# Packed chunks of attention: where the parts of keys and queries and the memory product are made

## The chip, the cores and the metric

The kernel runs on one core of a Trainium2 chip. The time is device microseconds of that core. The engines are named PE (TensorE), DVE (VectorE), ACT (ScalarE), POOL (GpSimd) and SP (SyncE, which issues most DMAs). Each takes its own instructions in the order in which they were issued to it; semaphores order them across engines.

## The reference

Attention with a memory term, and a top-2 mixture of experts on its result. B = 4 batches, H = 8 heads, S = 576 rows, D = 64; 2304 tokens of 512 values; 8 experts with 512 x 1024 and 1024 x 512 weights.

```
scores = q @ k^T / 8, causal; a = softmax(scores); local = a @ v
q_p    = where(q > 0, q, exp(q) - 1) + 1
mem    = (q_p @ M_prev) / (q_p . z_prev + 1e-6)
x      = sigmoid(beta) * mem + (1 - sigmoid(beta)) * local
logits = x @ w_gate + log1p(exp(x @ w_noise)) * noise; the two largest, softmax over them
out    = sum over the two experts of weight * (relu(x @ w1[e]) @ w2[e])
```

All is float32.

## The kernel before

**Precision.** A product that must be near float32 is made of three products of split operands: a high part (a copy into fp32r) and a low part (the float32 value minus the high part): high x high, low x high, high x low. So each operand needs one cast and one subtraction before it can be used.

**Attention.** A batch has 576 rows: four chunks of 128 rows (i = 0 to 3) and one of 64 (i = 4). Chunks are numbered c = 0 to 19, so the last ones of the batches are c = 4, 9, 14 and 19. These are packed: the 64 rows of two heads share the 128 partitions (`q4` tiles with zeros off the diagonal, one pair for all packed chunks), and their scores are made at line 519, with 576 keys in two halves of 288. The first half needs keys of older chunks only; the second needs the chunk's own 64 keys. Other chunks make their scores at line 528.

A chunk is worked in units of heads, two heads each for i of 2 or more. A step of the main loop (line 738) handles unit u: the exponentials of unit u + 1 (`expo`, line 559), the products with the values of unit u - 2 (`av`, line 599), the score products of unit u + 2 (`score`: `products`, then `tops`, which adds the mask and takes each row's negated maximum at line 538), and the transposes of unit u (`trans`, lines 577 and 578). Between them go the steps that prepare later chunks, by due times (lines 706 to 715): `q_turn` and `q_split`, `k_turn` with `k_split`, `q_min`, `phi`, `mem`. `in_turn` (line 726) ties TensorE's instructions to each other in exactly the order in which the steps were issued. The other engines keep the order of issue by their queues.

**The steps that the change touches.** `k_turn` transposes the keys on PE (line 409), ACT scales them into `kf` (line 416), and `k_split` makes the high part (line 421) and the low part (line 422) in the tile `kT`. `q_turn` makes `qf` (line 441); `q_split(0)` makes the high part (line 452) and `q_split(1)` the low part (line 454), for a packed chunk in two pieces of 64 x 256. `mem` makes the memory product, twice in a chunk with four heads each: PE (line 466), a copy by ACT (line 469), the divisor by DVE (lines 473 and 475), and the product into `xm` (line 476), which `out_turn` adds at line 639. From chunk 2 on, lines 421, 422, 452, 454 and 476 all run on POOL.

**Routing.** A finished chunk is scaled on DVE (lines 637 and 639), transposed (line 149) and multiplied with the gate weights (lines 160, 161); when a batch is finished, `routing` counts places with small DVE steps (line 196 and others), and writes ten rows of a table to DRAM by indirect DMAs that POOL issues (`put`, line 282). The steps of batch b are worked while batch b + 1 is in attention, and its puts fall into that batch's later chunks. After the puts of batch 2, `early` (line 837) loads the first table rows (`tabE`, by SP) and POOL gathers rows of x by them (`xw`, line 809); the experts' part begins with these (`xprep`, line 855).

**Experts.** Nine passes over the weights; PE makes lines 919 and 932, DVE, ACT and POOL split weights (lines 880 to 883), POOL gathers and scatters rows.

Of the kernel before, what the change touches and what calls it, by code (L numbers as in the profile page):

```python
# [9 lines left out]
F32 = mybir.dt.float32  # L10
# [5 lines left out]
ALU = mybir.AluOpType  # L16
# [25 lines left out]
def rows_of(i):  # L42
    return P if i < 4 else 64
# [3 lines left out]
def tile_attention_moe(ctx: ExitStack, tc: tile.TileContext, q, k, v, M_prev, z_prev, beta,  # L47
                       w_gate, w_noise, noise, w1, w2, out):
    nc = tc.nc
# [269 lines left out]
    def attention():  # L319
        with ExitStack() as c2:  # L320
# [71 lines left out]
            def prep(c):  # L392

                b, i = chunks[c]
                n = rows_of(i)
                d = CH.setdefault(c, {"b": b, "i": i, "n": n})
                t0 = i * P

                def keys():

                    if i == 0:
                        KT[b] = (ap_ if b % 2 else kp).tile([P, 2, 4, S], F32R, tag="kT", name="kT", bufs=1)
                    return [KT[b][:, x_, :, t0:t0 + n] for x_ in range(2)]
# [9 lines left out]
                def k_turn():  # L413
                    v_ = turn("k")
                    d["kf"] = ap_.tile([P, 4, P], F32, tag="kf", name="kf", bufs=2)[:, :, 0:n]
                    nc.scalar.activation(d["kf"], v_, AF.Copy, scale=0.125)
                    k_split()

                def k_split():
                    hi, lo = keys()  # L420
                    (nc.gpsimd.tensor_copy if c > 1 else nc.scalar.copy)(hi, d["kf"])
                    nc.gpsimd.tensor_tensor(out=lo, in0=d["kf"], in1=hi.bitcast(F32), op=ALU.subtract)

                def turn_first(nm, g0):

# [21 lines left out]
                def q_split(part):  # L447
                    for j in ([0, 1] if i == 4 else [None]):
                        a = slice(0, P) if j is None else slice(j * 64, j * 64 + 64)
                        hi, lo = [d[nm][a, :, a] for nm in ("qh", "ql")]  # L450
                        if part == 0:
                            (nc.gpsimd.tensor_copy if c > 1 else nc.scalar.copy)(hi, d["qf"][a])
                        else:
                            nc.gpsimd.tensor_tensor(out=lo, in0=d["qf"][a], in1=hi.bitcast(F32), op=ALU.subtract)

                def q_min():
                    d["qpT"] = ap_.tile([P, 4, P], F32, tag="qpT", name="qpT", bufs=2)
# [2 lines left out]
                def mem(g0):  # L460
                    if g0 == 0:
                        d["xm"] = ap_.tile([P, H, D], F32, tag="xm", name="xm", bufs=4)
                    tp = ps_tp.tile([P, 512], F32, tag="tp", name="tpm")
                    v_ = tp[0:n, 0:4 * 65].rearrange("p (h e) -> p h e", e=65)
                    for g in range(2):
                        nc.tensor.matmul(tp[0:n, g * 130:(g + 1) * 130], d["qpT"][:, g0 + g, 0:n],
                                         mz[:, b, g0 + g].rearrange("p a e -> p (a e)"), start=True, stop=True)
                    m_ = ap_.tile([P, 4 * 65], F32, tag="mm", name="mm", bufs=3)
                    nc.scalar.copy(m_[0:n], tp[0:n, 0:4 * 65])
                    v_ = m_[0:n].rearrange("p (h e) -> p h e", e=65)  # L470
                    r = ap_.tile([P, 4, 1], F32, tag="mr", name="mr", bufs=4)
                    hs = slice(2 * g0, 2 * g0 + 4)
                    nc.vector.scalar_tensor_tensor(out=r[0:n], in0=v_[:, :, 64:65], scalar=1e-6, in1=ig[0:n, hs].unsqueeze(2),
                                                   op0=ALU.add, op1=ALU.mult)
                    nc.vector.reciprocal(r[0:n], r[0:n])
                    nc.gpsimd.tensor_tensor(out=d["xm"][0:n, hs, :], in0=v_[:, :, 0:64],
                                            in1=r[0:n].to_broadcast([n, 4, 64]), op=ALU.mult)

                mm = [lambda: mem(0), lambda: mem(2)]
                qk = [lambda: q_split(0), lambda: q_split(1)]  # L480
                if c == 0:
                    return ([lambda nm=nm, g0=g0: turn_first(nm, g0) for g0 in (0, 2) for nm in "kq"],
# [255 lines left out]
            for u in range(NU + 2):  # L738
# [14 lines left out]
                if u < NU:  # L753
                    c, hs = units[u]
# [39 lines left out]
            d = CH[len(chunks) - 1]  # L794
# [413 lines left out]
```

## Time and profile before

| | |
|---|---|
| median of 3 runs | 780.79 us (780.27 to 782.5) |
| the profiled execution | 776.3 us, of which the span from first to last instruction is 774.6 |
| PE busy | 708.3 us, 91% |
| DVE | 418.1 us, 54% |
| ACT | 370.9 us, 48% |
| POOL | 364.2 us, 47% |

The page shows the span in 40 slices of 19.4 us. A digit is the busy share in tenths; PEclk is the granted clock of TensorE in tenths of full speed.

```profile
PE   6999995999599949988999999999999999999994
...
POOL 5534436433655360646453472662752753723602
PEclk7899997999799979999999999999999999999998
```

Read it by columns: in the 7th, 11th and 15th slice PE is only half busy and its clock is lower. Attention fills the first 16 slices, the experts the others. A timeline shows start and length of each instruction, or of a few of one kind; what stands in brackets is the engine's idle time before it and what released it.

### The profile page before, as it was taken

The page shows a single profiled execution, that of the slowest core. Times are in us where ns is not written, and L with a number is a line of the kernel's source. Part 1 is how long each engine was busy: PE and PEld are TensorE (multiplying, and loading weights), DVE is VectorE, ACT ScalarE, POOL GpSimd, SP SyncE. Part 2 cuts the span into 40 slices and gives each one's busy share as a digit, 9 for nine tenths or more (in the row PEclk, how much of TensorE's full clock was granted, in tenths as well). Part 3 has the DMA queues.
Part 4 walks back from the last instruction along what each step waited for, and adds up shares of the span by engine and source line. Part 5 has one row for each costly group of instructions (what it writes and reads, how often), then busy time and mean ns, then how long its engine had stood idle before and what let it go on. Part 6 is the DMA issues. An engine that isn't in the chain of part 4 may idle for free. (4 is left out here: it accounts for less than half of the span.)

```text
span 774.6 us, 14494 instructions
## 1 busy us (share of the span) xinstructions
PE 708.3 (91%) x5166; PEld 610.2 (79%) x5166; DVE 418.1 (54%) x1053; ACT 370.9 (48%) x951; POOL 364.2 (47%) x400
## 2 busy tenths in 40 slices
PE   6999995999599949988999999999999999999994
PEld 4778774877477737777888899988899888898883
DVE  3766683578367825945546454464554555455212
ACT  4887873797368736315525225235144144153110
POOL 5534436433655360646453472662752753723602
PEclk7899997999799979999999999999999999999998
DMA  8663521241120012559658466575594693864301
GB/s 162 104 145 89 112 56 36 62 97 55 36 63 22 29 41 84 153 120 224 192 106 208 143 150 162 161 191 119 183 200 106 191 213 111 219 146 144 101 1 61
DMA packets 165919, 92.95 MB, mean 120 GB/s; under 512 B 110564, under 2 KB 145380, under 8 KB 165840
## 3 DMA queue, kind: packets, MB, share of 16 engines
q1 hardware_dynamic: 155760, 72.97, 38.5%
q0 software_dynamic: 10080, 18.98, 9.7%
q8 instruction: 43, 0.70, 0.4%
q14 instruction: 36, 0.29, 0.1%
HBM read 69.68 MB, written 22.54 MB: 119 GB/s over the span
## 5 line engine op out<-in xcount | busy, mean ns | idle before, releaser
L881 POOL TENSOR_TENSOR w1lm<-w1sm,w1hm 128x512 fp32r<-128x512 f32 x63 | 81.9, 1303 | 131.3 <-DVE w1hm L880 71.5
L932 PE MATMUL y<-w2hm,hTh 128*128 128x512 f32 (+1 forms) x310 | 122.7, 396 | 0.0
L932 PE MATMUL y<-w2hm,hTl 128*128 128x512 f32 (+1 forms) x310 | 122.4, 395 | 0.0
L932 PE MATMUL y<-w2lm,hTh 128*128 128x512 f32 (+1 forms) x310 | 121.8, 393 | 0.0
L538 DVE TENSOR_REDUCE nb<-sc 128x1 f32<-128x384 f32 (+4 forms) x128 | 70.1, 557 | 64.0 <-PE sc L519 40.0
L922 ACT ACTIVATE hTh<-ha 128x304 fp32r<-128x304 f32 (+2 forms) x64 | 27.2, 425 | 159.3 <-PE ha L919 142.0
L882 ACT CAST w2hm<-w2sm 128x512 fp32r<-128x512 f32 x65 | 40.2, 620 | 99.5 <-PE y L932 98.6
L559 ACT ACTIVATE a<-sc,nb 128x128 f32<-128x128 f32 (+4 forms) x160 | 82.4, 529 | 8.9 <-DVE nb L538 5.2
L883 DVE TENSOR_TENSOR w2lm<-w2sm,w2hm 128x512 fp32r<-128x512 f32 x65 | 48.5, 746 | 54.4 <-ACT w2hm L882 54.0
L919 PE MATMUL hb<-xTh,w1hm 128*128 128x304 f32 (+1 forms) x236 | 71.8, 304 | 0.0
L880 DVE CAST w1hm<-w1sm 128x512 fp32r<-128x512 f32 x65 | 29.4, 452 | 78.2 <-PE hb L919 48.1
L919 PE MATMUL ha<-xTl,w1hm 128*128 128x304 f32 (+1 forms) x236 | 71.4, 303 | 0.0
L919 PE MATMUL ha<-xTh,w1hm 128*128 128x304 f32 (+1 forms) x236 | 71.2, 302 | 0.0
L919 PE MATMUL hb<-xTl,w1hm 128*128 128x304 f32 (+1 forms) x236 | 71.2, 302 | 0.0
L919 PE MATMUL hb<-xTh,w1lm 128*128 128x304 f32 (+1 forms) x236 | 70.9, 300 | 0.0
L919 PE MATMUL ha<-xTh,w1lm 128*128 128x304 f32 (+1 forms) x236 | 70.8, 300 | 0.0
L932 PEld LDWEIGHTS y<-w2hm,hTl 128*128 128x128 f32 (+1 forms) x310 | 56.8, 183 | 15.7 <-DVE hTl L923 0.5
L932 PEld LDWEIGHTS y<-w2lm,hTh 128*128 128x128 f32 (+1 forms) x310 | 57.0, 184 | 12.0
L577 PE MATMUL tpa<-identr,a 128*128 128x128 f32 x400 | 61.7, 287 | 4.9 <-ACT ll L170 4.3
L932 PEld LDWEIGHTS y<-w2hm,hTh 128*128 128x128 f32 (+1 forms) x310 | 57.0, 184 | 11.2
L578 ACT COPY aT<-tpa 128x512 f32<-128x512 f32 x120 | 58.0, 519 | 10.7 <-PE tpa L577 6.8
L599 PE MATMUL avT<-aT,vt 128*64 128x128 f32 (+1 forms) x960 | 60.3, 269 | 0.0
(250 smaller groups left out, 1639.0 us busy)
## 6 DMA issues: line engine op xcount, KB each, us to landing
w1sm<-in_moe_w_dram SPq DMA_DIRECT2D x65, 256.0 KB
w2sm<-in_moe_w_dram SPq DMA_DIRECT2D x65, 256.0 KB
y_scratch<-o SPq DMA_DIRECT2D x21, 256.0 KB
vt<-in_v_dram SPq DMA_DIRECT2D x16, 256.0 KB
xall_scratch<-xr SPq DMA_DIRECT2D x16, 256.0 KB
kn<-in_k_dram SPq DMA_DIRECT2D x15, 256.0 KB
qn<-in_q_dram SPq DMA_DIRECT2D x15, 256.0 KB
y_scratch<-o SPq DMA_DIRECT2D x14, 224.0 KB
```

What stands on the lines that cost most here:

```text
L538: nc.vector.tensor_reduce(out=nb[:, t * nh:(t + 1) * nh], in_=cols[t] if nh == 2 else cols[t][:, 0, :], axis=AX.X, op=ALU.max, negate=True)
L559: nc.scalar.activation(a[:, o:o + w], s_, AF.Exp, bias=st["nb"][:, x_:x_ + 1], accum_out=d["den"][:, at:at + 1])
L577: nc.tensor.transpose(tp[:, x_ * P:(x_ + 1) * P], a[:, (g + x_) * P:(g + x_ + 1) * P], ident)
L578: nc.scalar.copy(aT[:, g:g + w, :].rearrange("p b t -> p (b t)"), tp[:, 0:w * P])
L599: nc.tensor.matmul(o_[k_ * 64:(k_ + 1) * 64, h0 // 2, 0:n], CH[c0 + j]["v"][:, h0 + k_, :], r_, start=(j == 0), stop=(j == i))
L880: nc.vector.tensor_copy(h1, a)
L881: R["w1l"] = lo.tensor_tensor(out=l1, in0=a, in1=h1.bitcast(F32), op=ALU.subtract)
L882: nc.scalar.copy(h2, b_)
L883: nc.vector.tensor_tensor(out=l2, in0=b_, in1=h2.bitcast(F32), op=ALU.subtract)
L919: nc.tensor.matmul(o, w_[:, c, :], xT[xi][:, c, c0_:c1_], start=(c == 0 and i_ == 0), stop=(c == 3 and i_ == 2))
L922: R["hh"] = nc.scalar.activation(hT[0][:, c0_:c1_], o, AF.Relu)
L932: nc.tensor.matmul(ys[t][0:b_ - a_], hT[hi][:, a_:b_], w_, start=(f == 0 and i_ == 0), stop=(f == FF // P - 1 and i_ == 2))
```

## The change

In packed chunks (i = 4) the high parts of the keys and of the queries are made by ACT instead of POOL, and the low parts and the memory product by DVE instead of POOL. For one packed chunk that is one cast and one subtraction for the keys, two of each for the queries, and two memory products. The other chunks keep POOL, and the order of issue stays.

```diff
--- before.py
+++ after.py
@@ -418,8 +418,8 @@
 
                 def k_split():
                     hi, lo = keys()
-                    (nc.gpsimd.tensor_copy if c > 1 else nc.scalar.copy)(hi, d["kf"])
-                    nc.gpsimd.tensor_tensor(out=lo, in0=d["kf"], in1=hi.bitcast(F32), op=ALU.subtract)
+                    (nc.gpsimd.tensor_copy if c > 1 and i < 4 else nc.scalar.copy)(hi, d["kf"])
+                    (nc.gpsimd if i < 4 else nc.vector).tensor_tensor(out=lo, in0=d["kf"], in1=hi.bitcast(F32), op=ALU.subtract)
 
                 def turn_first(nm, g0):
 
@@ -449,9 +449,9 @@
                         a = slice(0, P) if j is None else slice(j * 64, j * 64 + 64)
                         hi, lo = [d[nm][a, :, a] for nm in ("qh", "ql")]
                         if part == 0:
-                            (nc.gpsimd.tensor_copy if c > 1 else nc.scalar.copy)(hi, d["qf"][a])
+                            (nc.gpsimd.tensor_copy if c > 1 and i < 4 else nc.scalar.copy)(hi, d["qf"][a])
                         else:
-                            nc.gpsimd.tensor_tensor(out=lo, in0=d["qf"][a], in1=hi.bitcast(F32), op=ALU.subtract)
+                            (nc.gpsimd if i < 4 else nc.vector).tensor_tensor(out=lo, in0=d["qf"][a], in1=hi.bitcast(F32), op=ALU.subtract)
 
                 def q_min():
                     d["qpT"] = ap_.tile([P, 4, P], F32, tag="qpT", name="qpT", bufs=2)
@@ -473,7 +473,7 @@
                     nc.vector.scalar_tensor_tensor(out=r[0:n], in0=v_[:, :, 64:65], scalar=1e-6, in1=ig[0:n, hs].unsqueeze(2),
                                                    op0=ALU.add, op1=ALU.mult)
                     nc.vector.reciprocal(r[0:n], r[0:n])
-                    nc.gpsimd.tensor_tensor(out=d["xm"][0:n, hs, :], in0=v_[:, :, 0:64],
+                    (nc.gpsimd if i < 4 else nc.vector).tensor_tensor(out=d["xm"][0:n, hs, :], in0=v_[:, :, 0:64],
                                             in1=r[0:n].to_broadcast([n, 4, 64]), op=ALU.mult)
 
                 mm = [lambda: mem(0), lambda: mem(2)]
```

## Rows read from the trace of the kernel before

**Rows 1.** Waits of TensorE, 0 to 300 us: engine, line, releaser, total us, times, longest

```profile
PE sc L519 <- POOL kT L421: 24.3, 3, 8.5
```

**Rows 2.** Timeline of GpSimd: start us, us, line, operation, tile, count, idle before

```profile
112.06 1.53 POOL L454 TENSOR_TENSOR q4l<-qf,q4h 64x256 fp32r<-64x256 f32 x2
...
116.94 1.19 POOL L282 DMA_INDIRECT tab_scratch<-rows,six  x1 [2.48 <-DVE rows L196]
...
128.88 0.90 POOL L282 DMA_INDIRECT tab_scratch<-rows,six  x1 [0.30 <-issue]
129.77 0.41 POOL L421 CAST kT<-kf 128x256 fp32r<-128x256 f32 x1
130.27 0.73 POOL L422 TENSOR_TENSOR kT<-kf,kT 128x256 fp32r<-128x256 f32 x1
```

**Rows 3.** Timeline of TensorE around packed chunks' first scores (four stretches)

```profile
57.51 0.53 PE L519 MATMUL sc<-kT,q4h 128*128 128x288 f32 x2
...
61.34 0.53 PE L519 MATMUL sc<-kT,q4h 128*128 128x288 f32 x2
...
74.49 0.33 PE L528 MATMUL sc<-kT,qh 64*128 64x128 f32 x2
...
121.36 0.40 PE L519 MATMUL sc<-kT,q4h 128*128 128x288 f32 x1
130.24 0.61 PE L519 MATMUL sc<-kT,q4h 128*128 128x288 f32 x1 [8.48 <-POOL kT L421]
...
136.65 0.54 PE L519 MATMUL sc<-kT,q4h 128*128 128x288 f32 x2
...
196.69 0.40 PE L519 MATMUL sc<-kT,q4h 128*128 128x288 f32 x1
...
211.57 0.53 PE L519 MATMUL sc<-kT,q4h 128*128 128x288 f32 x2
...
274.63 0.40 PE L519 MATMUL sc<-kT,q4h 128*128 128x288 f32 x1
282.93 0.61 PE L519 MATMUL sc<-kT,q4h 128*128 128x288 f32 x1 [7.91 <-POOL kT L421]
```

**Rows 4.** Three windows: length, busy us of each engine, PEclk, DMA share, GB/s

```profile
121.40:130.20 8.80, 0.35 (x3) 0.14 (x1) 0.09 (x1) 0.97 (x4) 6.96 (x8) 0.75 0.11 32
130.20:136.70 6.50, 6.46 (x39) 5.88 (x39) 2.94 (x9) 3.10 (x6) 2.83 (x3) 0.55 0.10 23
345.00:774.00 429.00, 411.63 (x2354) 365.70 (x2352) 204.01 (x379) 149.78 (x291) 205.14 (x200) 0.99 0.60 151
```

**Rows 5.** Timeline of ScalarE, 118 to 122 us

```profile
119.14 0.40 ACT L416 ACTIVATE kf<-tpk 128x256 f32<-128x256 f32 x1
...
120.92 0.69 ACT L559 ACTIVATE a<-sc,nb 128x512 f32<-128x512 f32 x1
```

**Rows 6.** Timeline of VectorE, 112 to 121.5 us

```profile
112.08 0.72 DVE L473 SCALAR_TENSOR_TENSOR mr<-mm,ib 128x4 f32<-128x4 f32 x1
...
117.23 2.09 DVE L538 TENSOR_REDUCE nb<-sc 128x1 f32<-128x512 f32 x3
...
120.80 0.69 DVE L639 TENSOR_TENSOR xr<-xr,xm 128x512 f32<-128x512 f32 x1
```

**Rows 7.** Groups by line and form: VectorE, then GpSimd; busy us, mean ns

```profile
L639 DVE TENSOR_TENSOR xr<-xr,xm 128x512 f32<-128x512 f32 x16 | 12.2, 760 | 1.0
...
L454 POOL TENSOR_TENSOR ql<-qf,qh 128x512 fp32r<-128x512 f32 x15 | 20.1, 1342 | 5.0 <-ACT qh L452 4.0
```

**Rows 8.** Timeline of GpSimd, 283 to 420 us

```profile
286.26 1.06 POOL L809 DMA_INDIRECT xw<-xall_scratch,tabE  x1 [2.58 <-DMA tabE<-tab_scratch]
...
345.17 1.04 POOL L809 DMA_INDIRECT xg<-xall_scratch,tall  x1 [4.33 <-DMA tall<-tab_scratch]
```

**Rows 9.** Timeline of TensorE, 295 to 352 us

```profile
301.80 0.60 PE L855 MATMUL tpm<-identr,xw 128*128 128x128 f32 x4
...
349.96 0.66 PE L855 MATMUL tpm<-identr,xg 128*128 128x128 f32 x4 [3.04 <-DMA xg<-xall_scratch,tall]
```

## The prediction

> **What bounds the kernel now.** I read the busy shares first: TensorE 91% over the whole span, no other engine above 54%. From 345 us on, in the experts' part, TensorE works 411.6 of 429 us at a granted clock of 0.99 [rows 4]; nothing that this change touches runs there, and an attention part that ends earlier moves all of it earlier. So the place to look is where TensorE stands still before that. The list of its waits has one entry that dwarfs the rest: the scores of packed chunks (line 519) waited three times, 24.3 us in total, for the GpSimd cast of line 421 that writes the high part of the keys [rows 1].
>
> The timelines show why. At chunk 9, GpSimd takes ten scatters of line 282 in a row (the first and the last are shown), from 116.94 to 129.78, and only then the cast, at 129.77, with no idle time ahead of it [rows 2]. ScalarE had its input ready long before: the scaled copy kf ran 119.14 to 119.54 [rows 5]. The cast did not wait for data; it waited for 10.2 us behind scatters that happen to stand ahead of it in GpSimd's queue. TensorE does the first score product at 121.36, whose keys are older, and then stands 8.48 us [rows 3]. In those 8.8 us the other two engines have nothing to do either: VectorE 0.09 us busy, ScalarE 0.97 [rows 4].
>
> The stall costs more than its length. In the 6.5 us after it TensorE is busy all the time, but at a granted clock of 0.55, which is about the lower of its levels (1.2 of 2.4 GHz); it had stood still just before [rows 4]. Chunk 4 is the control: the same steps, with no scatters ahead. From its first score product to that of its second unit it takes 61.34 - 57.51 = 3.83 us. Chunk 9 takes 136.65 - 121.36 = 15.29, chunk 14 takes 211.57 - 196.69 = 14.88 [rows 3].
>
> **The change, part by part.**
>
> *The stalls go.* Chunk 9 gives 15.29 - 3.83 = 11.46, chunk 14 gives 14.88 - 3.83 = 11.05. Chunk 19 has no such twin, because as the last chunk its steps are mixed otherwise. There I add the wait, 7.91 [rows 3], and what a window like the one at 130 us loses by the clock, 6.5 x (1 - 0.55) = 2.9 [rows 4]: 10.8. (Checked on chunk 9: 8.48 + 2.9 = 11.4.) Sum: 33.3 us.
>
> *The keys' new path.* The high part is now a ScalarE copy issued directly behind kf. No row has it; kf itself, 128x256, took 0.40 [rows 5], so it ends at about 119.9, and the subtraction on VectorE at about 120.3. TensorE wants the high part just after 121.4: 1.5 us of room.
>
> *What waits anew.* The subtraction sits in VectorE's queue, in order, and waits for that ScalarE copy. By the order in which the steps are issued, behind it stand two of the three row-maximum reductions that began at 117.23 and took 2.09 together [rows 6]. They now run from 120.3 to about 121.7 instead of ending at 119.3. The next exponential on ScalarE, at 120.92 [rows 5], needs the first of them, which ends at about 121.0; the one after it needs the second. Both come 0.1 us late. After that VectorE carries the scaling and addition of the previous chunk (the latter at 120.80 in the old order [rows 6]) some 1.5 us late, and TensorE turns that result soon after the first scores. Some tenths will show there.
>
> *Work added.* For one packed chunk: ScalarE three copies of 0.40 at most (the keys', two 64x256 for the queries) = 1.2. VectorE five operations (one for the keys, two for the queries, two for the memory product). The nearest row is the 128x512 addition with two inputs in SBUF, 0.76 on average [rows 7]; half the columns make 0.4 by estimate, so 2.0 in all. What covers it: TensorE's own products, for it is the engine that is busy in this stretch. What it costs when the cover is gone: 3.2 us for a chunk, all on the path. Where VectorE is crowded (112 to 119 us, with the routing steps of the batch before) there is something to gain as well: a 128x4 operation took 0.72 at 112.08 [rows 6], exactly while the first of GpSimd's two subtractions from 112.06 was running [rows 2], and those subtractions leave GpSimd.
>
> SBUF — State Buffer of the Trainium skill, section Who interferes with whom, says that a VectorE instruction with two SBUF inputs and a GpSimd instruction that reads SBUF block each other for a whole instruction. The trace agrees with it at 112.08. The same rule lets the new subtractions be held by GpSimd work beside them: with the longest such row, 1.34, once in each chunk, the sum would be 4 x 1.34 = 5.4 us worse, and without it nothing; it does not say that scatters hold them, and VectorE's addition at 120.80 took its 0.69 beside them.
>
> I take 0.5 us for a chunk, 2.0 for four, near the small lateness worked out above. Bounds: 3.2 x 4 = 12.8 worse with no cover; 1.4 better (two held operations released, each priced at the whole 0.72 of the one shown) in each of the three chunks with routing steps, so 4.3 better.
>
> *What is late next.* GpSimd still runs the ten scatters. Behind them now come the casts and subtractions of the two chunks that follow: queries twice (a subtraction 1.34 [rows 7], a cast about half) and the keys, together some 6 us after 129.8, so 135.8. TensorE wants the first of these for the next chunk's scores, which chunk 4's twin has 74.49 - 57.51 = 16.98 after its start [rows 3]: 138.3. It fits with 2.5 us of room, at no cost.
>
> At chunk 19 the gather of early rows hangs on the last scatter, not on TensorE. It starts at 286.26; a later gather took 349.96 - 345.17 = 4.8 us to be usable, so the rows are there at 291.1 [rows 8, 9]. The step that reads them ran at 301.80 [rows 9]; 10.8 earlier is 291.0. That is just in time; I cost it at 0, and 2 at most.
>
> Sum: 33.3 - 2.0 = 31.3. Against the profiled execution's own 776.3 us that makes 745.0. The median of the runs, 780.8, lies 4.5 above that execution; I let that difference stand, so 780.8 - 31.3 = 749.5.
>
> **Rivals.**
>
> *The queue moves on to the next chunk.* The scatters remain, and the chunks after 9 and 14 find their queries or keys late by 3 us, which TensorE pays with a low clock behind it: 2 x (3 + 2.9) = 11.8 back, 761.3. For it: the scatters' length is unchanged while TensorE arrives 11 us sooner. Against: the 2.5 us of room.
>
> *It doesn't do what it says.* If the wait is only put down to the cast and something else ends with it, nothing moves: 780.8. Against: in the stall no engine but GpSimd works, and the cast's end at 130.18 is followed by TensorE at 130.24 [rows 2, 3].
>
> *Slower: VectorE's queue closes a circle.* The subtraction waits for ScalarE, the reductions wait behind the subtraction, and ScalarE's exponentials wait for the reductions; if the ScalarE copy in turn comes to stand behind those exponentials, each packed chunk, chunk 4 too, pays a whole unit or more. From 33.3 / 4 = 8.3 us a chunk it decides; at 9 the time is 780.8 + 36 - 33.3 = 783.5. For it: VectorE is full before 119 us. Against: kf and the copy are issued next to each other, before the exponentials, so the circle is not closed.
>
> **How the numbers follow.** Forecast 0.80, next chunk late 0.13, no effect 0.03, slower 0.04. Everything within 0.3% (2.3 us) of 780.8 counts as the same: that is about what a measurement of this kernel can tell. Faster: 0.80 + 0.13 = 0.93; same 0.03; slower 0.04. The range goes from 780.8 - 33.3 - 4.3 = 743.2 to the uncovered bound, 780.8 - 33.3 + 12.8 = 760.3, and with the gather's 2, 762.
>
> **What would show it.** In the changed profile: line 421 on ScalarE directly behind line 416 in packed chunks, and no wait of line 519 for it over 1 us; a granted clock near 1 behind the first scores of chunks 9, 14 and 19, with 4 to 5 us from the first unit to the second; reductions of line 538 that stand behind the keys' subtraction; scatters still in one row; the next chunk's scores without a wait for GpSimd. I am wrong if TensorE stands over 3 us at those places for another engine, or if chunk 4 is several us longer than before.

## The result, and the profile after

The changed kernel takes 746.77 us (median of 3 runs, 742.02 to 747.23) against 780.79: a ratio of 0.954 (95% interval 0.948 to 0.961). Two more rounds of six runs each, beside other kernels, gave 0.959 (0.955 to 0.964) and 0.957 (0.952 to 0.962). One run each of the two kernels in the second of them was slow and is left out; by medians these rounds show 746.99 against 779.79 us and 746.15 against 779.19, that is 32.8 and 33.0 us less. The profiled execution took 747.23 us with a span of 745.5, that is 29.1 less span than before.

The page's slices of the changed kernel, TensorE and its clock:

```profile
PE   6999899999999878889999999999999999999993
...
PEclk7899999999999999989999999999999999999997
```

The half-busy columns with a low clock are gone. The waits of TensorE in the first 300 us (engine, tile, line, releaser, total, times, longest):

```profile
PE tpl L161 <- DVE xTll L153: 4.0, 6, 2.1
PE tpa L577 <- ACT ll L170: 3.4, 3, 1.3
PE tpo L635 <- ACT xo L608: 2.5, 4, 0.8
```

The line 519 entry, 24.3 us before [rows 1], is not there at all; what leads now is a wait of line 161 (1.8 us before) that the prediction did not have. The first score products of the packed chunks, and the first ones of the chunk after chunk 9, on TensorE's timeline (start, length):

```profile
57.94 0.54 PE L519 MATMUL sc<-kT,q4h 128*128 128x288 f32 x2
...
61.77 0.53 PE L519 MATMUL sc<-kT,q4h 128*128 128x288 f32 x2
...
124.61 0.53 PE L519 MATMUL sc<-kT,q4h 128*128 128x288 f32 x2
...
128.43 0.53 PE L519 MATMUL sc<-kT,q4h 128*128 128x288 f32 x2
...
141.80 0.33 PE L528 MATMUL sc<-kT,qh 64*128 64x128 f32 x2
...
188.15 0.54 PE L519 MATMUL sc<-kT,q4h 128*128 128x288 f32 x2
...
191.98 0.53 PE L519 MATMUL sc<-kT,q4h 128*128 128x288 f32 x2
...
252.39 0.53 PE L519 MATMUL sc<-kT,q4h 128*128 128x288 f32 x2
...
257.77 0.54 PE L519 MATMUL sc<-kT,q4h 128*128 128x288 f32 x2
```

They answer to [rows 3]. From a packed chunk's first scores to its second unit: 3.83 us in chunk 4 (3.83 before), 3.82 in chunk 9 (15.29), 3.83 in chunk 14 (14.88), 5.38 in chunk 19 (282.93 was still in the first unit; its second one began at 290.54, 15.91 after the first). Two windows of the changed kernel (length, busy time of PE, PEld, DVE, ACT and POOL, granted clock, DMA share, GB/s):

```profile
124.60:131.00 6.40, 6.40 (x60) 5.71 (x59) 4.22 (x13) 5.31 (x15) 4.88 (x6) 1.00 0.25 67
309.00:742.00 433.00, 417.20 (x2371) 370.48 (x2369) 205.38 (x380) 149.76 (x291) 205.68 (x200) 0.98 0.60 151
```

Behind chunk 9's first scores TensorE is now busy for the whole 6.4 us at a granted clock of 1.00, where it had been 0.55 [rows 4]; behind those of chunks 14 and 19 (188.10 to 194.00 and 252.30 to 259.00) it is 1.00 too. The experts' part is as full as before: 417.2 of 433 us against 411.6 of 429 [rows 4].

### The profile page after: what moved, and what is told of

It reads as the page before. It is cut to its first block, busy times and chain, and to the rows that moved or that the text cites. A ratio compares the mean times of both kernels' runs of the same rounds, so it can differ in the third digit from the quotient of the medians.

```text
span 745.5 us, 14446 instructions
## 1 busy us (share of the span) xinstructions
PE 700.6 (94%) x5166; PEld 603.4 (81%) x5166; DVE 422.5 (57%) x1073; ACT 374.4 (50%) x963; POOL 347.3 (47%) x368
## 3 DMA queue, kind: packets, MB, share of 16 engines
q0 software_dynamic: 10080, 18.98, 10.2%
## 5 line engine op out<-in xcount | busy, mean ns | idle before, releaser
L559 ACT ACTIVATE a<-sc,nb 128x128 f32<-128x128 f32 (+4 forms) x160 | 82.6, 531 | 11.4 <-DVE nb L538 6.7
L577 PE MATMUL tpa<-identr,a 128*128 128x128 f32 x400 | 59.2, 278 | 5.1 <-ACT ll L170 3.4
L1001 DVE COPY pl<-xg 128x512 uint16<-128x512 uint16 x70 | 41.4, 639 | 38.1 <-DMA trn<-pl 26.2
```

The lines of the kernel that those rows point to most:

```text
L559: nc.scalar.activation(a[:, o:o + w], s_, AF.Exp, bias=st["nb"][:, x_:x_ + 1], accum_out=d["den"][:, at:at + 1])
L577: nc.tensor.transpose(tp[:, x_ * P:(x_ + 1) * P], a[:, (g + x_) * P:(g + x_ + 1) * P], ident)
L1001: nc.vector.tensor_copy(pl[:, h_], xv[:, h_])
```

## The experiments

The theory: the keys' cast waited for its place in GpSimd's queue, behind the ten scatters. Rivals: that GpSimd's work as such, or its port shared with VectorE, was the cost; or that something else ended with the wait. Each kernel was timed beside the kernel before, on one chip for each group of runs. The edits are shown shortened; `<order only>` stands for a dependency that only orders two instructions.

**e1: the keys alone.** Only `k_split` is changed.

```diff
-(nc.gpsimd.tensor_copy if c > 1 else nc.scalar.copy)(hi, d["kf"])
-nc.gpsimd.tensor_tensor(out=lo, ...)
+(nc.gpsimd.tensor_copy if c > 1 and i < 4 else nc.scalar.copy)(hi, d["kf"])
+(nc.gpsimd if i < 4 else nc.vector).tensor_tensor(out=lo, ...)
```

> Only the keys' two parts of packed chunks are moved; queries and memory product stay on GpSimd. Theory (queue position: the cast waited behind ten scatters): the three stalls go, 33 us, so within 2 us of the full change, 745 to 750. Rival (GpSimd is slow or in VectorE's way, and any work taken off it helps in proportion): the keys are 1.1 of 4.8 us of GpSimd work per packed chunk, so about a quarter of the gain, near 772.

Measured: 746.24 us, ratio 0.961 (0.955 to 0.966). TensorE at chunk 9:

```profile
122.37 0.53 PE L519 MATMUL sc<-kT,q4h 128*128 128x288 f32 x2
...
126.20 0.53 PE L519 MATMUL sc<-kT,q4h 128*128 128x288 f32 x2
```

From the first scores to the second unit it takes 3.83 us here and in chunk 14, and 5.39 in chunk 19, as in the changed kernel. Within the noise the keys carry the whole gain.

**e2: the queries and the memory product alone.** The other edits of the change, keys as before.

```diff
-(nc.gpsimd.tensor_copy if c > 1 else nc.scalar.copy)(hi, d["qf"][a])
+(nc.gpsimd.tensor_copy if c > 1 and i < 4 else nc.scalar.copy)(hi, d["qf"][a])
...
+(nc.gpsimd if i < 4 else nc.vector).tensor_tensor(out=lo, in0=d["qf"][a], ...)
...
+(nc.gpsimd if i < 4 else nc.vector).tensor_tensor(out=d["xm"][0:n, hs, :], ...)
```

> Only the queries' parts and the memory product of packed chunks are moved; the keys stay on GpSimd. Theory: the scatters still stand ahead of the keys' cast, three waits of about 8 us at line 519 remain, 778 to 783. Rival (work taken off GpSimd): three quarters of the gain, near 755.

Measured: 779.14 us, ratio 1.000 (0.997 to 1.003). The wait stands where it stood, each a little over 1 us shorter:

```profile
PE sc L519 <- POOL kT L421: 20.8, 3, 7.3
```

From first scores to second unit chunks 9, 14 and 19 take 14.26, 14.43 and 15.80 us, against 15.29, 14.88 and 15.91 before. Three quarters of the GpSimd work moved, and no gain that the runs can tell from none. The rival of e1 and e2 is out.

**e3: no engine changed, only the order.** The steps that issue the scatters are held until the packed chunk's `k_split` has been issued, and each scatter is ordered behind its subtraction. (`f.after` names the batch whose packed chunk has to be past that point.)

```diff
-steps.append(lambda i=i, w=w: puts.append(lambda: put(i, w)))
+f = lambda i=i, w=w: puts.append(lambda: put(i, w))
+f.after = min(b + 1, B - 1)
+steps.append(f)
...
+tc.add_manual_dep(s_.ins, R["klo"][1].ins.name, <order only>)
```

> No step changes its engine: all as before, on GpSimd, but the ten table scatters are put behind the packed chunk's key subtraction in GpSimd's queue. Theory: the stalls go by the order alone, 745 to 753 (the gather of early rows in chunk 19 may come 1 or 2 us later and cost that). Rival (the engine matters, not its queue): no change, 778 to 783.

Measured: 756.36 us, ratio 0.974 (0.970 to 0.978). The order alone gives 22.6 us; the cause is shown. It does not give all. Its GpSimd, around chunk 9 (line numbers are shifted by 4 to 6 in this kernel: 425 is the cast of 421, 525 the scores of 519, 534 those of 528):

```profile
120.91 0.40 POOL L425 CAST kT<-kf 128x256 fp32r<-128x256 f32 x1 [5.15 <-ACT kf L420]
...
122.36 1.49 POOL L282 DMA_INDIRECT tab_scratch<-rows,six  x1 [0.25 <-DMA kn<-in_k_dram]
...
136.26 0.90 POOL L282 DMA_INDIRECT tab_scratch<-rows,six  x1 [0.30 <-issue]
...
140.21 1.07 POOL L425 CAST kT<-kf 128x512 fp32r<-128x512 f32 x1
```

and its TensorE:

```profile
122.66 0.53 PE L525 MATMUL sc<-kT,q4h 128*128 128x288 f32 x2
...
126.49 0.53 PE L525 MATMUL sc<-kT,q4h 128*128 128x288 f32 x2
...
141.33 0.33 PE L534 MATMUL sc<-kT,qh 64*128 64x128 f32 x2 [2.17 <-POOL kT L425]
...
278.89 0.88 PE L866 MATMUL tpm<-identr,xw 128*128 128x128 f32 x4 [3.67 <-DMA xw<-xall_scratch,tabE]
```

The cast comes before the scatters, and the packed chunk runs at full pace (126.49 - 122.66 = 3.83). Then the next chunk pays: the scatters end at 137.2, the packed chunk's memory products and the next chunks' queries follow, the keys' cast is at 140.21, and TensorE waits 2.17 us for it, and less for the parts after it. At the end, the early gather hangs on the last scatter and TensorE waits 3.67 us for its rows. The prediction had weighed both for the change itself, the first as a rival, the second as a term of 0 to 2 us; in this kernel, where the scatters start later and the packed chunk's work is still in the queue, they came true. In the list of TensorE's waits to 300 us they are 3.6 us for the cast of line 425, 3.6 for the subtraction behind it (1.4 in the changed kernel) and 3.7 for the gather: 9.5 us more, of the 10.1 by which e3 is slower than e1.

**e4: the high part alone.**

```diff
-(nc.gpsimd.tensor_copy if c > 1 else nc.scalar.copy)(hi, d["kf"])
+(nc.gpsimd.tensor_copy if c > 1 and i < 4 else nc.scalar.copy)(hi, d["kf"])
```

> Only the high part of packed chunks' keys is made by ScalarE; the low part stays on GpSimd behind the scatters. Theory: TensorE gets two product pairs further and then waits for the low part, about 8 us three times, put down to the line of the subtraction; 777 to 782, almost nothing won. Rival (it was the cast's own latency on GpSimd): 747 to 765.

Measured: 776.99 us, ratio 1.000 (0.997 to 1.002). The wait is now for the subtraction, and as long; the list of waits, then TensorE at chunk 9:

```profile
PE sc L519 <- POOL kT L422: 23.7, 3, 8.3
```

```profile
123.11 0.29 PE L519 MATMUL sc<-kT,q4h 128*128 128x288 f32 x1
131.71 0.61 PE L519 MATMUL sc<-kT,q4h 128*128 128x288 f32 x1 [8.31 <-POOL kT L422]
```

Both parts have to leave the queue; TensorE gets as far as the last pair of products and stops in the middle of it.

**e6: all chunks.** Keys' and queries' parts of every chunk on ScalarE and VectorE (from the changed kernel).

```diff
-(nc.gpsimd.tensor_copy if c > 1 and i < 4 else nc.scalar.copy)(hi, ...)
-(nc.gpsimd if i < 4 else nc.vector).tensor_tensor(out=lo, ...)
+nc.scalar.copy(hi, ...)
+nc.vector.tensor_tensor(out=lo, ...)
```

> Keys' and queries' parts of all chunks on ScalarE and VectorE, memory product of unpacked chunks still on GpSimd. Theory: what helped was to leave the queue behind the scatters, and the other chunks don't wait in it, so nothing more is won, and some 20 us of added work on each of the two engines shows in part: 745 to 760. Rival (work taken off GpSimd helps by itself): under 742.

Measured: 747.31 us, ratio 0.959 (0.954 to 0.963), the same within the noise as the changed kernel beside it (746.99). Nothing won by freeing GpSimd further, and no price of the added work that an interval of this width can tell; in the profiled execution, the slowest of the six (753.88), line 161 waits more:

```profile
PE tpl L161 <- DVE xTll L153: 7.0, 8, 2.6
```

**e8: the stall filled.** The kernel before, with products of no use in the place of the stall.

```diff
+if c > 4 and g == 0 and x_ == 0 and t == 1:
+    for _ in range(76):
+        nc.tensor.matmul(banks[1][:, 288:512], warm[:, 0:P], warm[:, 0:224], start=True, stop=True)
```

> The kernel before, with 76 small products (bf16, 224 columns, into columns that nobody reads) put into TensorE's order at the place of each of the three stalls, so that it works while it waits, with nothing else changed. Theory (about 2.9 us of each stall's price is the low clock behind it, because TensorE stood still): the clock stays near 1 there, 769 to 775. Rival (the clock falls for another reason, or costs nothing): 778 to 783.

Measured: 774.0 us, ratio 0.993 (0.991 to 0.996): 5.8 us less than before by doing more. TensorE at chunk 9 (line numbers are shifted here: 521 is the filling, 522 the scores of 519), and the window behind the stall:

```profile
125.99 0.40 PE L522 MATMUL sc<-kT,q4h 128*128 128x288 f32 x1
126.23 7.46 PE L521 MATMUL sc<-warm 128*128 128x224 bf16 x76
134.87 0.40 PE L522 MATMUL sc<-kT,q4h 128*128 128x288 f32 x1 [1.18 <-POOL kT L421]
...
138.86 0.53 PE L522 MATMUL sc<-kT,q4h 128*128 128x288 f32 x2
```

```profile
134.80:141.00 6.20, 6.11 (x53) 5.19 (x54) 3.70 (x8) 4.02 (x10) 2.72 (x4) 1.00 0.10 21
```

It still has to wait for the keys (1.18 us after the filling), and goes on 134.87 - 125.99 = 8.88 us after the first score product, exactly as before (130.24 - 121.36 [rows 3]). But the clock is 1.00 behind it instead of 0.55 [rows 4], and from the first scores to the second unit it takes 138.86 - 125.99 = 12.87 instead of 15.29. In chunk 14 it is 12.29 instead of 14.88, in chunk 19 13.84 instead of 15.91. So 2.4, 2.6 and 2.1 us of the stalls' price were the clock.

**after_again, after_third, e7 and e9: the new wait.** In the changed kernel's profile VectorE waits 3.92 us in chunk 4 for `dB`, a 1 KB transfer that brings half of the row sums to the other partitions, and TensorE stands behind it. VectorE and TensorE of the changed kernel:

```profile
80.94 0.15 DVE L631 SCALAR_TENSOR_TENSOR ar<-dB,ib 64x4 f32<-64x4 f32 x1 [3.92 <-DMA dB<-d]
```

```profile
82.53 0.29 PE L161 MATMUL tpl<-xTll,wgs 128*16 128x128 f32 x1 [2.10 <-DVE xTll L153]
```

the same VectorE step before:

```profile
78.88 0.16 DVE L631 SCALAR_TENSOR_TENSOR ar<-dB,ib 64x4 f32<-64x4 f32 x1 [2.26 <-DMA dB<-d]
```

and VectorE and TensorE of the changed kernel in another execution (span 739.8):

```profile
77.48 0.15 DVE L631 SCALAR_TENSOR_TENSOR ar<-dB,ib 64x4 f32<-64x4 f32 x1 [2.25 <-DMA dB<-d]
```

```profile
79.07 0.23 PE L161 MATMUL tpl<-xTll,wgs 128*16 128x128 f32 x1 [0.43 <-DVE xTll L153]
```

The same program waits 3.92 in one execution and 2.25 in the other; TensorE's share of that is 2.10 and 0.43. In chunk 4 this is not the change: e8, whose chunk 4 is that of the kernel before, waits 3.70 there, and the length differs from one execution to the next. Chunk 19 is another matter: the step waits 3.18 us there (at 274.31; 3.05 and 3.08 in the two repeats), where the kernel before waited for nothing, and TensorE stands 1.13 us for the VectorE step of line 171 behind it. e7 orders the VectorE step behind the row maxima of its step, e9 does the same with the keys alone changed.

```diff
 x_ = nc.vector.scalar_tensor_tensor(out=rv[:, :, t], in0=s_, ...)
+if t == 1:
+    tc.add_manual_dep(x_.ins, R["top"].ins.name, <order only>)
```

> The changed kernel once more, beside the others on one chip: 742 to 748. In chunk 4 and the other packed chunks VectorE waits for the 1 KB transfer dB, a different time in each run.

> The changed kernel with one order edit: the VectorE step that reads the transfer dB (line 631, second half) stands behind the row maxima of its step instead of ahead of other work. Theory (the 3 us lost in chunk 4 of the changed kernel come from VectorE's queue standing still for that transfer): the wait of TensorE at line 161 falls from 2.1 to 0.5 us, 2 to 4 us less than the changed kernel beside it, 739 to 745. Rival (the wait only shows where something else is late): the same as the changed kernel within 1 us.

> The full change, to pair with the two others on one chip: 744 to 748.

> The full change with the late step once more, beside the full change: 1 to 3 us less than it if the transfer's wait is on the path, the same within 1 us if not.

> Only the keys' parts of packed chunks moved, and the VectorE step that reads the transfer dB put behind the row maxima. Theory (the keys carry the whole gain; the transfer costs about 2 us where VectorE's queue stands still for it): 743 to 746, as the full change with the late step, and 1 to 3 us under the full change. Rival (the queries' and memory parts gain something of their own, by the shared port): 2 us or more above the full change with the late step.

Measured: the changed kernel 746.99 and 746.15; e7 745.4 and 744.49, ratios 0.958 (0.953 to 0.962) and 0.957 (0.952 to 0.962); e9 744.78, ratio 0.957 (0.952 to 0.961). In e7 the step of chunk 4 runs without any wait, some 8 us later:

```profile
88.71 0.12 DVE L631 SCALAR_TENSOR_TENSOR ar<-dB,ib 64x4 f32<-64x4 f32 x1
```

and line 161's wait of 2 us is gone from its profile. But 1.6 and 1.7 us between medians, with intervals of 0.009 to 0.010 in the ratio, are not resolved: the medians lie on the side that was expected, twice. e9 shows no loss against e7. None of these is shown to beat the changed kernel.

The stages tell more than the medians. The table has, from the trace of each run, VectorE's wait for `dB` in chunk 4, then TensorE's time from chunk 4's first scores to the product of line 599 (602 in e8) that follows the transposes of chunk 4's output (line 635), and from there to chunk 9's first scores (all in us):

| run | wait for dB | chunk 4 | on to chunk 9 |
|---|---|---|---|
| before | 2.26 | 31.07 | 32.78 |
| e8 | 3.70 | 34.02 | 32.77 |
| e1 | 3.63 | 32.38 | 32.77 |
| e2 | 3.75 | 34.11 | 32.61 |
| changed | 3.92 | 34.08 | 32.59 |
| after_again | 3.48 | 33.79 | 32.61 |
| after_third | 2.25 | 31.03 | 32.60 |
| e7 | none | 30.44 | 32.96 |
| e7_again | none | 30.43 | 32.94 |
| e9 | none | 30.40 | 33.15 |

Without the wait chunk 4 takes 30.4 us three times, with it 31.0 to 34.1, before the change as after it: in this stage the late step does what was expected, and gives some 0.35 us back on the way to chunk 9. The queries' parts and the memory product, taken off GpSimd, give 0.2 us on the way to chunk 9, in pairs with and without the late step alike: too little for the medians to show.

## Why the prediction was right

**The stalls go.** 11.46, 11.05 and 10.8 were predicted; 15.29 - 3.82 = 11.47, 14.88 - 3.83 = 11.05 and 15.91 - 5.38 = 10.53 came, 33.05 us in all against 33.3. Chunk 4 as the control is what made this exact: it already showed what the steps take without scatters ahead.

**The split into wait and clock.** 2.9 us of clock for a stall were worked out; e8 measured 2.4, 2.6 and 2.1 in the stages, and 5.8 / 3 = 1.9 by the medians. The direction is shown, the size was somewhat high. That the check on chunk 9, 8.48 + 2.9 = 11.4, came out is luck: with the clock up the stall still makes the stage 12.87 - 3.83 = 9.04 us longer (e8), so the parts are 9.0 and 2.4, one half a microsecond above its estimate and the other as much below.

**The keys' new path.** ScalarE in the changed kernel, chunk 9:

```profile
122.40 0.40 ACT L416 ACTIVATE kf<-tpk 128x256 f32<-128x256 f32 x1
122.82 0.41 ACT L421 CAST kT<-kf 128x256 fp32r<-128x256 f32 x1
```

The copy follows the scaling directly and takes 0.41, as predicted from the 0.40 [rows 5]. TensorE asks for it at 124.6, some 1.4 us after its end (1.5 predicted).

**What waits anew: wrong in its order, without harm.** VectorE in the same stretch, then TensorE:

```profile
115.53 0.15 DVE L473 SCALAR_TENSOR_TENSOR mr<-mm,ib 128x4 f32<-128x4 f32 x1
...
116.31 0.60 DVE L196 SCALAR_TENSOR_TENSOR ov<-pos,ov 128x40 f32<-128x40 f32 x1
...
120.54 2.08 DVE L538 TENSOR_REDUCE nb<-sc 128x1 f32<-128x512 f32 x3
123.26 0.43 DVE L422 TENSOR_TENSOR kT<-kf,kT 128x256 fp32r<-128x256 f32 x1 [0.64 <-ACT kT L421]
```

```profile
120.67 0.46 PE L409 MATMUL tpk<-identr,kn 64*128 64x64 f32 x4
121.06 0.29 PE L534 MATMUL sc<-mask,identb 128*128 128x128 bf16 x2
```

The prediction put two of the three reductions behind the subtraction, from the order in which the code issues the steps. They ran ahead of it (120.54 to 122.62), and the subtraction after them, with 0.64 us of waiting. TensorE, whose order is that of the steps, transposes the keys at 120.67 and adds the masks for the last two reductions at 121.06, so the code does issue these two behind the keys. VectorE's queue is not in the order in which the code issues the steps, contrary to what is said ahead of the prediction; only TensorE's order is fixed by hand. So the reductions came no later, and in place of 1.5 us VectorE was 0.34 late with the previous chunk's result: its addition, line 639, starts at 124.39, 0.22 ahead of the first scores, where it had been 0.56 ahead (120.80 and 121.36 [rows 3, 6]).

The term of half a microsecond for a chunk, 2.0 in all, did not show. The product of line 599 ahead of chunk 9's preparation, before and after:

```profile
88.58 0.66 PE L599 MATMUL avT<-aT,vt 128*64 128x128 f32 x8
```

```profile
92.02 0.66 PE L599 MATMUL avT<-aT,vt 128*64 128x128 f32 x8
```

TensorE, 3.44 later there, was only 3.25 later at chunk 9's first scores: that chunk's preparation cost nothing and gave 0.19 back, and the table has this in every execution. That chunk 4's first scores came 0.43 later than before says nothing: in the repeats of the changed kernel they stand at 56.30 and 56.16, earlier than before.

**The shared port.** The 128x4 operation of line 473, which took 0.72 beside a GpSimd subtraction [rows 6], takes 0.15 at 115.53 with GpSimd idle, and a small one of line 196 takes 0.60 at 116.31 while GpSimd's memory product of 116.11 (0.75 long) runs. By the rule of the Trainium skill, SBUF — State Buffer, section Who interferes with whom, a VectorE instruction with two SBUF inputs contends with a GpSimd instruction that reads SBUF; both rows agree with it. The table fits as well: with the queries and the memory product on GpSimd the way to chunk 9 takes 32.77 or 32.78 us (before, e1, e8), without them 32.59 to 32.61 (e2, the changed kernel three times). That the port is the whole of this 0.2 us is argued from the rows, not tested by a run.

**The next chunk and the gather.** GpSimd of the changed kernel around chunk 9:

```profile
116.11 0.75 POOL L476 TENSOR_TENSOR xm<-mm,mr 128x256 f32<-128x256 f32 x1 [3.76 <-ACT lt L163]
120.24 1.19 POOL L282 DMA_INDIRECT tab_scratch<-rows,six  x1 [3.38 <-DVE rows L196]
...
131.79 1.17 POOL L282 DMA_INDIRECT tab_scratch<-rows,six  x1 [0.30 <-issue]
132.96 0.63 POOL L452 CAST qh<-qf 128x512 fp32r<-128x512 f32 x1
...
137.81 1.29 POOL L422 TENSOR_TENSOR kT<-kf,kT 128x512 fp32r<-128x512 f32 x1
```

The scatters start 3.3 us later and end at 133.0; queries and keys of the next chunks follow at once, the keys' low part ends at 139.1, and TensorE wants it at 141.80: 2.7 us of room, 2.5 predicted. In e3, where the scatters end 137.16 - 122.66 = 14.5 us after the first scores instead of 132.96 - 124.61 = 8.35, that room is used up. The early gather started at 265.62 and TensorE read its rows at 269.09 without waiting for them, so the 4.8 us taken from a later gather were too many; "just in time" was right, for in after_again TensorE waits 0.19 us for them.

**The sum.** 749.5 us was predicted and 746.77 measured, a gain of 34.0 between medians against 31.3, and 32.8 and 33.0 in the later rounds: about the stalls' 33.05, with next to nothing paid for them. Between the two profiled executions it was 29.1. To the stalls' 33.05 come 2.65 saved between chunk 14's second unit and chunk 19's first scores (63.06 before, 60.41 after; a wait of 0.87 where 1.80 had brought the clock down, 0.79 from 220 to 228 us); 3.01 were lost in chunk 4 with the transfer, 3.45 between the gather for the experts' part (345.17 before [rows 8], 312.62 after) and the end, and 0.14 in the rest. The first three of these are of the execution, not of the change: in the two repeats of the changed kernel the stretch ahead of chunk 19 takes 60.45 and 63.19, chunk 4 takes 33.79 and 31.03, and the stretch to the end 433.2 and 429.7, with 432.9 in the profiled execution and 429.4 before. So the prediction's sign of being wrong, a chunk 4 several us longer than before, did appear in this execution, but for the transfer's sake. Executions of the changed kernel spread over 741 to 750 us.

## What to carry to other kernels

When an instruction is late, compare the time at which its input was ready with the time at which it started, and look at what its own queue did in between: here 10.2 us of a finished input behind ten unrelated transfers. Then move only what TensorE waits for (the two key steps were all of the gain), or reorder the queue, but count what lands behind the transfers instead, for e3 got two thirds of it and paid the rest to the next in line. A repeated stage that lacks the disturbance prices the whole stall, low clock included, better than the wait's own length.

## What the runs showed of the hardware that was not expected

- A stall of 8 us costs TensorE 2.1 to 2.6 us more afterwards by the clock, granted at 0.55 behind it and at 1.00 with useless products in its place (e8); these win that back, 5.8 us between medians for three.
- The 1 KB transfer between partitions landed 1.8 to 5.4 us after its issue within one execution of the changed kernel, and chunk 4 takes 31.03 to 34.08 us with it from one execution to the next, 30.4 where TensorE doesn't stand behind it (e7, e9).
- VectorE took 31 subtractions of 128x512 more and ScalarE 28 casts, with no change of the time that the runs could tell (e6: 0.959 with an interval of 0.954 to 0.963).
